# Unit 0 in two halves, and three weights met in plain fp32, in a fused attention and MLP kernel

## The chip, the cores and the metric

The kernel runs on one core of a Trainium2 chip. The metric is the device time of one execution in microseconds (us). The core has five engines that work side by side and meet by semaphores: TensorE (PE, matrix products; PEld is its weight load), VectorE (DVE), ScalarE (ACT), GpSimd (POOL) and SyncE (SP, which here issues the transfers). Each engine takes its instructions strictly in the order in which the program lists them.

## The reference

A linear attention with decay feeds a two-layer MLP.

```python
# r, k, v, w: batch 4, heads 8, steps 768, head size 48; u: heads x 48
for t in range(S):
    cur = einsum('bhd,bhe->bhde', u[None] * kt, vt)
    y[:, :, t] = einsum('bhd,bhde->bhe', rt, state + cur)
    state = wt[:, :, :, None] * state + einsum('bhd,bhe->bhde', kt, vt)
x = y as 3072 tokens x 384
h = x @ w_in                      # 384 x 2048
g = where(h >= 1, h, where(h <= -1, 0, (h + 1)**2 / 4))
out = g @ w_out                   # 2048 x 384
```

The data are fp32; the MLP weights come as 64-bit words and are turned into fp32 on the chip.

## The kernel before

**Units and blocks.** The sequence is cut into 12 units of 64 steps by 4 batches (256 tokens). Two units make a block of 512 tokens; there are six blocks. The eight heads lie as four pairs; a row tile `q` (0 or 1) holds two pairs.

**Attention of a unit** (`attention(u)`). VectorE makes two running products of the decays per row tile with scans (L451 back, L456 forward), and scales `k` (L474, called at L488) and `r` (L474, called at L550) with them. TensorE then makes the scores inside the unit, twice: the diagonal with `u * k` (`among`, tenant `bd`, L508) and the part below it (`among`, tenant `ba`, L508). VectorE copies each set of scores under a mask into `r_` (`picked`, L516). TensorE also transposes `k` (L558), multiplies the scores with `v` (`along`, L618), forms the state update (`umat`, L583), moves the rows of the fourth head pair beside the other three (`spread`, L709, with the permutation `perm` that POOL builds from the constants at L443), and subtracts the rounded part of x (`less`, L699). ScalarE reads x out of PSUM twice, as its high part (L688) and its low part (L684). For units 0 and 1 ScalarE also multiplies `k` with `u` (L479) before the diagonal scores.

**Weights** (`weight(f)`, 16 tiles of 128 hidden columns). A transfer brings the words (L335). ScalarE converts the upper word (L347) into one of three fp32 buffers `fl` and the lower word (L352); VectorE adds signs (L366) and joins both (L369). Then the fp32 tile is split: the high part `w_hi` (L343 on ScalarE, L341 on VectorE for two of them) and the rest `w_lo` (L373, VectorE). A buffer of `fl` is free for the weight three further on when `w_lo` has been made.

**Products** (`products(n)`). Every product of x with a weight is made of three single-pass products of type fp32r: high by high, high by low, low by high. So one weight tile and one block half take nine matmuls into the hidden tile (`product_in`, L1262) and nine out of it (`product_out`, L1282). Between them stand the activation: two ScalarE passes (L1062, L1063), a minimum and maximum on VectorE (L1072), and the split of g into high (L1074, ScalarE) and low (L1075, VectorE). In block 0 the first five weights are done by halves of 256 tokens: for unit 0 the steps (0), (1, 2), (3, 4).

**Order.** The program first lists all operations with their reads and writes. `ORDER` is then a written-out permutation of that list, which fixes the order on every engine; `BANKS` gives each PSUM tenant its bank; `FILLS` names places in TensorE's order where products with a tile of zeros are put in (operation, bank, columns). The first transfers in SP's order are: decays and r, k of row tile 1, decays of row tile 0, decays of unit 1, the mask `below`, r, k of row tile 0, the constants `cst` (seventh), weights 0, 1 and 2, and `v` of unit 0. They are 261.5 KB for the decays of a row tile, 512 KB for its r and k, 32 KB for `below`, 96 KB for `cst`, 768 KB for a weight and 384 KB for `v`. The final three blocks use a scheme with fewer products (L932), which the change leaves as it is.

Of the kernel before, what the change touches and what calls it, by code (L numbers as in the profile page):

```python
# [22 lines left out]
UT = 256  # L23
# [109 lines left out]
)  # L133
FILLS = (
    (42, 0, 256, False), (50, 0, 512, False), (54, 0, 384, False),
)

LOW = 7.499 * 2.0**-32


class Plan:
# [26 lines left out]
    def emits(self, fill):  # L168

        put_in = {n: x for n, *x in FILLS}  # L170
        for n in ORDER:
            if n in put_in:
                fill(*put_in[n])
            self.ops[n]["emit"]()
# [1171 lines left out]
```

## Time and profile before

| | us |
|---|---|
| median of three runs | 486.84 |
| lowest, highest | 486.79, 489.51 |
| profiled execution: span | 489.6 |
| PE busy | 470.8 (96%) |
| PEld busy | 417.4 (85%) |
| DVE busy | 403.1 (82%) |
| ACT busy | 301.8 (62%) |
| POOL busy | 28.1 (6%) |

The page gives the profiled execution's own time only as its span, 489.6 us, near the highest of the three runs. A row of the timeline gives the start, the duration, the engine, the line and the operation; in brackets stands how long the engine had been idle before it and what ended that. Rows of one engine can overlap by a few tenths at their ends, because a matmul or a copy runs out while the next one starts.

### The profile page before, as it was taken

The page shows a single profiled execution, that of the slowest core. Times are in us where ns is not written, and L with a number is a line of the kernel's source. Part 1 is how long each engine was busy: PE and PEld are TensorE (multiplying, and loading weights), DVE is VectorE, ACT ScalarE, POOL GpSimd, SP SyncE. Part 2 cuts the span into 40 slices and gives each one's busy share as a digit, 9 for nine tenths or more (in the row PEclk, how much of TensorE's full clock was granted, in tenths as well). Part 3 has the DMA queues.
Part 4 walks back from the last instruction along what each step waited for, and adds up shares of the span by engine and source line. Part 5 has one row for each costly group of instructions (what it writes and reads, how often), then busy time and mean ns, then how long its engine had stood idle before and what let it go on. Part 6 is the DMA issues. An engine that isn't in the chain of part 4 may idle for free.

```text
span 489.6 us, 13368 instructions
## 1 busy us (share of the span) xinstructions
PE 470.8 (96%) x5709; PEld 417.4 (85%) x5709; DVE 403.1 (82%) x627; ACT 301.8 (62%) x582; POOL 28.1 (6%) x49
## 2 busy tenths in 40 slices
PE   2899999999999999999999999999999999999994
PEld 2689888889999999888888888999889999889984
DVE  6899999999897888798998977889687657585682
ACT  4788988854635276365655567855846656776560
POOL 4000000000000000000000033412300000000000
PEclk9999999999999999999999999999999999999998
DMA  8939646324650435243444201110010111121102
GB/s 317 384 134 325 263 174 205 105 70 147 199 169 3 148 111 170 100 168 105 149 154 138 85 3 50 46 23 15 9 39 28 45 23 21 33 76 44 23 1 72
DMA packets 35205, 53.53 MB, mean 109 GB/s; under 512 B 15744, under 2 KB 22592, under 8 KB 35136
## 3 DMA queue, kind: packets, MB, share of 16 engines
q1 hardware_dynamic: 34992, 52.45, 32.3%
q8 instruction: 47, 0.77, 0.7%
q14 instruction: 22, 0.18, 0.1%
q10 hardware_dynamic: 144, 0.13, 0.1%
HBM read 46.86 MB, written 4.72 MB: 105 GB/s over the span
## 4 chain that ended last, share of the span: by engine, by line
PE 85%; DVE 5%; DMA 5%; issue 2%; SPq 2%; ACT 1%; DVEq 0%
PE ps L1262 37%; PE ps L932 19%; PE ps L1282 18%; PE ps L618 4%; PE ps L508 3%; PE ps L558 2%; DMA rk<-in_rk 2%; DMA wq<-in_w 2%; PE ps L583 2%; DMA nk<-in_nk 1%; DVE y L451 1%; SPq L730 1%; SPq L280 1%; DVE fl L369 1%; DVE rk L474 0%
## 5 line engine op out<-in xcount | busy, mean ns | idle before, releaser
L1262 PE MATMUL ps<-x,wt 128*128 128x512 f32 (+1 forms) x1035 | 214.0, 357 | 0.1
L1262 PEld LDWEIGHTS ps<-x,wt 128*128 128x128 f32 x1035 | 168.1, 188 | 26.8 <-DVE rk L894 0.4
L1282 PE MATMUL ps<-gh,wt 128*128 128x256 f32 (+1 forms) x402 | 79.3, 332 | 0.4 <-DVE g L1072 0.4
L1282 PEld LDWEIGHTS ps<-gh,wt 128*128 128x128 f32 x402 | 61.5, 188 | 7.9 <-DVE g L1072 0.6
L892 ACT ACTIVATE rk<-ps 128x512 f32<-128x512 f32 x48 | 28.4, 597 | 46.3 <-PE ps L1262 27.3
L894 DVE SCALAR_TENSOR_TENSOR rk<-rk,ps 128x512 f32<-128x512 f32 x48 | 32.6, 684 | 24.1 <-ACT rk L893 23.9
L1062 ACT ACTIVATE g<-ps 128x512 f32<-128x512 f32 (+1 forms) x49 | 28.7, 588 | 34.7 <-PE ps L1262 23.1
L1282 PE MATMUL ps<-gl,wt 128*128 128x256 f32 (+1 forms) x201 | 44.1, 328 | 0.0
L1074 ACT CAST gh<-g 128x512 fp32r<-128x512 f32 (+1 forms) x49 | 29.5, 609 | 18.4 <-DVE g L1072 18.4
L1072 DVE SCALAR_TENSOR_TENSOR g<-g,ps 128x512 f32<-128x512 f32 (+1 forms) x49 | 32.2, 665 | 6.3 <-ACT g L1063 6.3
L1075 DVE TENSOR_TENSOR gl<-g,gh 128x512 fp32r<-128x512 f32 (+1 forms) x49 | 32.9, 678 | 4.1 <-ACT gh L1074 3.9
L1282 PEld LDWEIGHTS ps<-gl,wt 128*128 128x128 f32 x201 | 32.3, 188 | 3.6
L451 DVE TENSOR_TENSOR_SCAN y<-wq,ends 128x520 f32<-128x520 f32 x24 | 29.6, 1234 | 5.5 <-POOL r L289 3.8
L900 DVE TENSOR_TENSOR g_again<-rk,nk_again 128x512 fp32r<-128x512 f32 x35 | 24.5, 711 | 11.3 <-ACT nk_again L899 11.2
L900 DVE TENSOR_TENSOR gl<-rk,gh 128x512 fp32r<-128x512 f32 x36 | 25.1, 704 | 9.6 <-ACT gh L899 9.5
L1063 ACT ACTIVATE g<-g 128x512 f32<-128x512 f32 (+1 forms) x49 | 30.0, 622 | 0.4
L893 ACT ACTIVATE rk<-rk 128x512 f32<-128x512 f32 x48 | 29.4, 630 | 0.5
L456 DVE TENSOR_TENSOR_SCAN p<-wq,seeds 128x520 f32<-128x520 f32 x24 | 29.7, 1237 | 0.0
L899 ACT CAST gh<-rk 128x512 fp32r<-128x512 f32 x36 | 22.1, 617 | 7.7 <-DVE rk L918 3.9
L899 ACT CAST nk_again<-rk 128x512 fp32r<-128x512 f32 x35 | 21.5, 617 | 5.7 <-DVE rk L894 3.5
L932 PE MATMUL ps<-nk_again,wt 128*128 128x256 f32 x130 | 24.9, 281 | 0.0
L851 POOL TENSOR_TENSOR p<-wt 128x256 f32<-128x256 f32 x8 | 6.9, 873 | 294.0 <-DVE p L851 294.0
(165 smaller groups left out, 842.5 us busy)
## 6 DMA issues: line engine op xcount, KB each, us to landing
rk<-in_rk SPq DMA_DIRECT2D x18, 512.0 KB, 4.1
wraw<-in_wbits SPq DMA_DIRECT2D x11, 768.0 KB, 6.2
nk<-in_nk SPq DMA_DIRECT2D x9, 768.0 KB, 4.6
wq<-in_w SPq DMA_DIRECT2D x24, 261.5 KB, 3.5
wraw<-in_wbits SPq DMA_DIRECT2D x15, 256.0 KB, 5.9
vn<-in_v SPq DMA_DIRECT2D x9, 384.0 KB, 4.6
rk<-in_rk SPq DMA_DIRECT2D x12, 256.0 KB, 5.8
last<-in_w SPq DMA_DIRECT2D x12, 256.0 KB, 3.0
```

The lines of the kernel that those rows point to most:

```text
L451: V.tensor_tensor_scan(out=y_[:, ::-1], data0=w[:, SEG:0:-1], data1=ends.rearrange("p n c -> p (n c)")[:, ::-1], initial=0.0, op0=ALU.mult ...
L456: V.tensor_tensor_scan(out=pv[:, q].rearrange("p n c -> p (n c)"), data0=w[:, 0:SEG], data1=sv, initial=0.0, op0=ALU.mult, op1=ALU.add)
L894: op("DVE", 0.68, [("b", ht)], [qk], lambda: V.scalar_tensor_tensor(out=gf, in0=gf, scalar=1.0, in1=at(ht), op0=ALU.min, op1=ALU.max))
L899: op("ACT", 0.6, [key], fresh_in(("h", i, k)), lambda: A.copy(spare(k, i), x))
L900: op("DVE", 0.67, [key, ("h", i, k)], fresh_in(("l", i, k)), lambda: V.tensor_tensor(out=spare(k, 3 + i), in0=x, in1=spare(k, i).bitcast(F ...
L932: PE.matmul(at(sums_at[b][i])[:, half * UT : half * UT + UT], lhsT=w[wi], rhs=g[gi], start=(b, i) not in opened, stop=True, skip_group_che ...
L1063: op("ACT", c, (), [("g", gk)], lambda: A.activation(gs, gs, AF.Square))
L1072: op("DVE", 0.15 + 0.53 * k, [("b", ht)], [("g", gk)], lambda: V.scalar_tensor_tensor(out=gs, in0=gs, scalar=1.0, in1=hs(), op0=ALU.min, o ...
L1074: op("ACT", c, [("g", gk)], [("gh", gk)], lambda: A.copy(ghs, gs))
L1075: op("DVE", 0.145 + 0.54 * k, [("g", gk), ("gh", gk)], [("gl", gk)], lambda: V.tensor_tensor(out=gls, in0=gs, in1=ghs.bitcast(F32), op=ALU ...
L1262: nc.tensor.matmul(hp, lhsT=wx[f][:, cs], rhs=xt[:, j, :], start=first and n == 0, stop=n == 8, skip_group_check=not first)
L1282: nc.tensor.matmul(o[j], lhsT=wx[f][:, cs], rhs=gt, start=first and i == 0, stop=stop and i == 2, skip_group_check=True)
```

## The change

It does four things.

- **Unit 0 in halves.** The scores of unit 0, their masked copies and the product with `v` are each made in two halves, first head pairs 2 and 3 (row tile 1), then pairs 0 and 1 (row tile 0). The fourth head pair is then spread before the second half of `along`.
- **Three weights in plain fp32.** For unit 0, weights 0, 1 and 2 are multiplied straight from the fp32 buffers `fl`, with x in fp32 (a new copy `x32`, ScalarE) and g in fp32, three plain fp32 matmuls in and three out in place of nine and nine. The split of g (L1074, L1075) falls away for these two steps. `w_hi` and `w_lo` of these weights are still made, for the other tokens.
- **A new order.** `ORDER` and `BANKS` are new as a whole. Among the first transfers `cst` is now fourth, `v` of unit 0 comes ahead of weight 2, and the decays of unit 1 come tenth. On POOL `seeds` is set second and one half of `r_` only after `perm`.
- **Six fills in place of three**: 1920 columns of zeros in all, where 1152 were. They stand ahead of the transpose of row tile 1 (896 columns), its diagonal scores (128), the first half of `along` (640) and the second half (256), all in unit 0.

```diff
+PARTED = {0}
+PLAIN = {0, 1, 2}
 FILLS = (
-    (42, 0, 256, False), (50, 0, 512, False), (54, 0, 384, False),
+    (46, 3, 512, False), (46, 3, 384, False), (38, 3, 128, False), (54, 0, 512, False), (54, 0, 128, False), (55, 2, 256, False),
 )
...
+        if early and parted:
+            bd = plan.tenant(2)
+            for q in (1, 0):
+                op("PE", 0.48, [("ku", q), "nk", ("r", slot[q])], [("bq", bd, q)], lambda q=q: among(
+                    bd, lambda q: ku[:, q], lambda q: raw(q, 0), mine(q)), code=64, small=True, touch=[bd])
+                op("DVE", 0.7, [("bq", bd, q), "cst"], R_of(q), lambda q=q: picked_of(bd, twice.bitcast(I32), q), touch=[bd])
...
+        if parted and u == 0:
+            op("PE", 0.48, [*R_of(1), vk, ("vpad", 0), rs[1]], [("b", by)], lambda: along((2,)), fresh=False, code=64, small=True)
+            op("PE", 0.48, [*R_of(0), vk, ("vpad", 0), rs[0]], [("bq", by, 0)], lambda: along((0,)), fresh=False, code=64, small=True, touch=[by])
...
+        if u == 0:
+            op("ACT", 0.8, [("b", by), ("bq", by, 0)], ["x32"], lambda: A.copy(
+                x32.rearrange("p a (c g t) -> p a c g t", c=2, g=2), two(by).rearrange("p g (a c t) -> p a c g t", a=4, t=C)[:, 0:3]))
...
+        plain = b == 0 and cs == halves[0] and set(fs) <= PLAIN
+        for i, f in enumerate(fs if plain else ()):
+            op("PE", 1.4, [("fl", f % FULL), "x32", *after], [("b", ht)], lambda i=i, f=f: product_in_f32(
+                nc, at(ht)[:, i * w : i * w + w], fl[f % FULL], x32, not i), fresh=not i, code=12)
...
-            op("ACT", c, [("g", gk)], [("gh", gk)], lambda: A.copy(ghs, gs))
+            if not plain:
+                op("ACT", c, [("g", gk)], [("gh", gk)], lambda: A.copy(ghs, gs))
...
+            if plain:
+                op("PE", 1.4, [("g", gk), ("fl", f % FULL)], [("b", acc[j]) for j in range(3)], fresh=begin, code=12,
+                   emit=lambda f=f, mine=mine, begin=begin: product_out_f32(
+                       nc, [at(t)[:, cs] for t in acc], fl[f % FULL], gs[:, mine], begin))
+                continue
...
+def product_in_f32(nc, hp, s, x, first=True):
+    for n, j in enumerate((2, 0, 1)):
+        nc.tensor.matmul(hp, lhsT=s[:, j * 128 : j * 128 + 128], rhs=x[:, j, :], start=first and n == 0, stop=n == 2, skip_group_check=not first)
```

The numbers in `op(...)` are the planner's own costs; they do not reach the chip.

## Rows read from the trace of the kernel before

**Rows 1.** The page, busy time of each engine (share of the span) and instructions.
```profile
PE 470.8 (96%) x5709; PEld 417.4 (85%) x5709; DVE 403.1 (82%) x627; ACT 301.8 (62%) x582; POOL 28.1 (6%) x49
```

**Rows 2.** Windows: PE, PEld, DVE, ACT, POOL busy (instructions); clock, DMA share, GB/s.
```profile
10.00:20.00 10.00, 9.54 (x219) 6.95 (x218) 8.67 (x12) 7.24 (x13) 1.65 (x2) 1.00 1.02 392
20.00:50.00 30.00, 27.88 (x563) 25.23 (x561) 29.85 (x41) 26.05 (x47) 0.00 (x0) 1.00 0.72 250
50.00:60.00 10.00, 10.00 (x115) 9.13 (x108) 9.47 (x15) 9.05 (x14) 0.00 (x0) 1.00 0.77 309
60.00:100.00 40.00, 40.00 (x426) 33.33 (x425) 39.78 (x57) 31.49 (x52) 0.00 (x0) 1.00 0.46 154
100.00:200.00 100.00, 99.44 (x1643) 93.55 (x1641) 89.48 (x122) 49.92 (x100) 0.00 (x0) 1.00 0.38 124
200.00:480.00 280.00, 279.76 (x2731) 245.59 (x2730) 217.72 (x373) 174.47 (x352) 22.25 (x30) 1.00 0.20 60
```

**Rows 3.** Timeline of PE, 0 to 50 us, lines of the front.
```profile
8.72 1.09 PE L558 MATMUL ps<-cst,xf 128*128 128x128 f32 x4 [8.72 <-DVE xf L474]
...
10.48 1.99 PE L508 MATMUL ps<-rk,nk 64*64 64x64 f32 x64
...
15.23 1.13 PE L298 MATMUL ps<-zero 128*128 128x512 f32 x2
...
18.45 1.58 PE L709 MATMUL ps<-ob,nk 128*128 128x128 f32 x12
...
26.09 0.66 PE L558 MATMUL ps<-cst,rk 128*128 128x128 f32 x4 [0.61 <-DVE rk L474]
...
32.38 0.67 PE L618 MATMUL ps<-rk,st 64*48 64x64 f32 x32
...
38.20 3.39 PE L1262 MATMUL ps<-x,wt 128*128 128x256 f32 x27
41.44 0.87 PE L1282 MATMUL ps<-gh,wt 128*128 128x256 f32 x6
...
49.64 1.33 PE L508 MATMUL ps<-rk,nk 64*64 64x64 f32 x64 [0.63 <-ACT nk L479]
```

**Rows 4.** Timeline of DVE, 12 to 41 us, lines that the change touches or moves.
```profile
12.70 1.31 DVE L516 COPY_PREDICATED r<-cst,ps 128x1024 f32<-128x1024 int32 x1 [0.47 <-ACT wraw L352]
...
15.37 1.30 DVE L516 COPY_PREDICATED r<-below,ps 128x1024 f32<-128x1024 int32 x1 [0.86 <-PE ps L508]
...
22.80 0.56 DVE L341 CAST wt<-fl 128x768 fp32r<-128x768 f32 x1
...
30.35 0.95 DVE L373 TENSOR_TENSOR wt<-fl,wt 128x768 fp32r<-128x768 f32 x1
31.21 1.33 DVE L516 COPY_PREDICATED r<-below,ps 128x1024 f32<-128x1024 int32 x1
...
35.13 0.42 DVE L1072 SCALAR_TENSOR_TENSOR g<-g,ps 128x256 f32<-128x256 f32 x1
...
36.33 0.42 DVE L1075 TENSOR_TENSOR gl<-g,gh 128x256 fp32r<-128x256 f32 x1
...
38.13 0.67 DVE L1072 SCALAR_TENSOR_TENSOR g<-g,ps 128x512 f32<-128x512 f32 x1
...
39.88 0.67 DVE L1075 TENSOR_TENSOR gl<-g,gh 128x512 fp32r<-128x512 f32 x1
```

**Rows 5.** Waits for the constants, POOL's timeline, 8 to 12 us.
```profile
8.72 0.70 POOL L443 COPY nk<-cst 128x32 f32<-128x32 f32 x1 [5.03 <-DMA cst<-in_consts]
```

**Rows 6.** SP's issue of v of unit 0, from the timeline.
```profile
5.93 0.69 SPq L280 DMA_DIRECT2D vn<-in_v  x1
```

**Rows 7.** Transfers issued from 0 to 60 us: count, KB each, us to landing.
```profile
vn<-in_v SPq DMA_DIRECT2D x1, 384.0 KB, 9.4
```

**Rows 8.** Timeline of ACT, 20 to 26 us.
```profile
20.19 0.79 ACT L688 CAST x<-ps 128x768 fp32r<-128x768 f32 x1
...
25.39 0.91 ACT L347 ACTIVATE fl<-wraw 128x768 f32<-128x768 f32 x1 [0.90 <-DVE wt L373]
```

More of the change, by code (lines that the diff above doesn't have):

```diff
@@ L145, in __init__, with add @@
         self.tenants, self.where = [], BANKS
-    def add(self, engine, cost, emit, reads=(), writes=(), port=0, size=0, fresh=True, code=0, small=False):
+    def add(self, engine, cost, emit, reads=(), writes=(), port=0, size=0, fresh=True, code=0, small=False, touch=()):
         n = len(self.ops)
+        for t in touch:
+            self.tenants[t]["users"].append(n)
         deps = {self.writer[x] for x in (*reads, *writes) if x in self.writer}
@@ L168, in emits @@
     def emits(self, fill):
-        put_in = {n: x for n, *x in FILLS}
+        put_in = {}
+        for n, *x in FILLS:
+            put_in.setdefault(n, []).append(x)
         for n in ORDER:
-            if n in put_in:
-                fill(*put_in[n])
+            for x in put_in.get(n, ()):
+                fill(*x)
             self.ops[n]["emit"]()
@@ L288, in attention_moe @@
         for h in range(2):
-            op("POOL", 0.5, (), [("R", h)], lambda h=h: G.memset(r_[:, h], 0.0))
+            op("POOL", 0.5, (), [("R", h, q) for q in range(2)], lambda h=h: G.memset(r_[:, h], 0.0))
     last_f = ob[:, 0:UT]
@@ L394, in bonus @@
             nc.sync.dma_start(out=u_sb[:, cs], in_=a["us"][:, cs])
-    aside_keys = {1: [("aside", 1, 1)], 2: [("aside", 0, 0), ("aside", 0, 1), ("aside", 1, 0)]}
+    x32 = flat(xf[1], 512, 1280).rearrange("p (a t) -> p a t", t=UT)
+    aside_keys = {1: [("aside", 1, 1), "x32"], 2: [("aside", 0, 0), ("aside", 0, 1), ("aside", 1, 0)]}
     def attention(u):
@@ L496, in attention, with among @@
         dv = d_.rearrange("p c (a h) -> p h a c", h=2)
-        def among(to, left, right):
-            for pair in range(4):
+        def among(to, left, right, pairs=range(4)):
+            for pair in pairs:
                 q, pr = divmod(pair, 2)
@@ L511, in among @@
                             )
-        both_R = [("R", 0), ("R", 1)]
+        both_R = [("R", h, q) for q in range(2) for h in range(2)]
         def picked(of, mask):
@@ L518, in picked, with picked_of, R_of, mine @@
                 data=two(of).rearrange("p h (n c) -> p (h n) c", c=C))
-        if early:
+        def picked_of(of, mask, q):
+            V.copy_predicated(
+                out=r_[:, :, 2 * q : 2 * q + 2].rearrange("p h a b c -> p h (a b) c"),
+                mask=mask.unsqueeze(1).unsqueeze(1).broadcast_to([128, 2, 4, C]),
+                data=two(of)[:, :, 256 * q : 256 * q + 256].rearrange("p h (n c) -> p h n c", c=C))
+        def R_of(q):
+            return [("R", h, q) for h in range(2)]
+        def mine(q):
+            return range(2 * q, 2 * q + 2)
+        parted = u in PARTED
+        if early and parted:
[4 more added lines that the diff above has]
+                op("DVE", 0.7, [("bq", bd, q), "cst"], R_of(q), lambda q=q: picked_of(bd, twice.bitcast(I32), q), touch=[bd])
+        elif early:
             bd = plan.tenant(2)
@@ L545, in attention @@
             for h in range(2):
-                op("DVE", 0.68, ["d", "cst"], [("R", h)], lambda h=h: V.tensor_tensor(
+                op("DVE", 0.68, ["d", "cst"], [("R", h, q) for q in range(2)], lambda h=h: V.tensor_tensor(
                     out=r_[:, h], in0=twice.unsqueeze(1).unsqueeze(1).broadcast_to([128, 4, 2, C]),
@@ L558, in ktrans @@
                     PE.transpose(out=at(b)[:, lo : lo + 128], in_=ready(q, 1)[:, tokens(pr, c2)], identity=ident)
-        op("PE", 0.95, [*ks, *rs], [("b", ba)],
-           lambda: among(ba, lambda q: ready(q, 1), lambda q: ready(q, 0)), code=128, small=True)
+        if parted:
+            for q in (1, 0):
+                op("PE", 0.48, [ks[q], rs[q]], [("bq", ba, q)], lambda q=q: among(
+                    ba, lambda q: ready(q, 1), lambda q: ready(q, 0), mine(q)), code=64, small=True, touch=[ba])
+        else:
+            op("PE", 0.95, [*ks, *rs], [("b", ba)],
+               lambda: among(ba, lambda q: ready(q, 1), lambda q: ready(q, 0)), code=128, small=True)
         goes_on = u < NU - 1
@@ L568, in attention @@
                     kt[:, 2 * q : 2 * q + 2].rearrange("p a b c -> p (a b c)"), at(b)))
-        op("DVE", 1.32, [("b", ba), "below"], both_R, lambda: picked(ba, below))
+        if parted:
+            for q in (1, 0):
+                op("DVE", 0.7, [("bq", ba, q), "below"], R_of(q), lambda q=q: picked_of(ba, below, q), touch=[ba])
+        else:
+            op("DVE", 1.32, [("b", ba), "below"], both_R, lambda: picked(ba, below))
         bu = plan.tenant(2) if goes_on else None
@@ L635, in cross, with along @@
             crossed(1)
-        def along():
+        def along(ones=(0, 2)):
             if u:
                 crossed(0)
-            for one_ in (0, 2):
+            for one_ in ones:
                 for c2 in range(2):
@@ L662, in attention @@
                 op("DVE", 0.94, [("b", bu), ("s", now)], [("s", new)], step)
-        op("PE", 1.42 if u else 0.95, [*ss, *both_R, vk, ("vpad", u % 2), *rs], [("b", by)], along, fresh=False, code=192 if u else 128, small=True)
+        if parted and u == 0:
+            op("PE", 0.48, [*R_of(1), vk, ("vpad", 0), rs[1]], [("b", by)], lambda: along((2,)), fresh=False, code=64, small=True)
+            op("PE", 0.48, [*R_of(0), vk, ("vpad", 0), rs[0]], [("bq", by, 0)], lambda: along((0,)), fresh=False, code=64, small=True, touch=[by])
+        else:
+            op("PE", 1.42 if u else 0.95, [*ss, *both_R, vk, ("vpad", u % 2), *rs], [("b", by)], along, fresh=False,
+               code=192 if u else 128, small=True)
         blk, half = divmod(u, 2)
@@ L717, in attention @@
         parts_x = 1 if flat_x else 2
+        if u == 0:
+            op("ACT", 0.8, [("b", by), ("bq", by, 0)], ["x32"], lambda: A.copy(
+                x32.rearrange("p a (c g t) -> p a c g t", c=2, g=2), two(by).rearrange("p g (a c t) -> p a c g t", a=4, t=C)[:, 0:3]))
         for what in (0,) if alone else (1, 0):
-            op("ACT", 0.37 if what else 0.8, [("b", by)], [names(what, 0), *(() if what else aside_keys.get(blk, ()))], lambda w=what: yevac(0, w))
+            op("ACT", 0.37 if what else 0.8, [("b", by), ("bq", by, 0)], [names(what, 0), *(() if what else aside_keys.get(blk, ()))], lambda w=what: yevac(0, w))
             if u not in INPLACE and not flat_x:
@@ L819, in attention_moe @@
     st_keys = [[("spad", i), ("s", i)] for i in range(2)]
-    R_keys = [("R", 0), ("R", 1)]
+    R_keys = [("R", h, q) for q in range(2) for h in range(2)]
     olds = [(("w", 0),), (("w", 1),), (("w", 2),), ("y",), ("seeds",), *[fl_keys] * 4, R_keys, R_keys, *[vn_keys] * 3, *st_keys]
@@ L1057, in products @@
         x = x_[b % 2]
-        for i, f in enumerate(fs):
+        plain = b == 0 and cs == halves[0] and set(fs) <= PLAIN
+        for i, f in enumerate(fs if plain else ()):
+            op("PE", 1.4, [("fl", f % FULL), "x32", *after], [("b", ht)], lambda i=i, f=f: product_in_f32(
+                nc, at(ht)[:, i * w : i * w + w], fl[f % FULL], x32, not i), fresh=not i, code=12)
+        for i, f in enumerate(() if plain else fs):
             op("PE", 2.1 * kw, [("wh", f), ("wl", f), *x_keys(b, cs), *after], [("b", ht)], lambda i=i, f=f: product_in(
@@ L1073, in products @@
                 out=gs, in0=gs, scalar=1.0, in1=hs(), op0=ALU.min, op1=ALU.max))
-            op("ACT", c, [("g", gk)], [("gh", gk)], lambda: A.copy(ghs, gs))
-            op("DVE", 0.145 + 0.54 * k, [("g", gk), ("gh", gk)], [("gl", gk)], lambda: V.tensor_tensor(
-                out=gls, in0=gs, in1=ghs.bitcast(F32), op=ALU.subtract), port=True)
+            if not plain:
+                op("ACT", c, [("g", gk)], [("gh", gk)], lambda: A.copy(ghs, gs))
+                op("DVE", 0.145 + 0.54 * k, [("g", gk), ("gh", gk)], [("gl", gk)], lambda: V.tensor_tensor(
+                    out=gls, in0=gs, in1=ghs.bitcast(F32), op=ALU.subtract), port=True)
         acc = sums_at[b]
@@ L1098, in attention_moe @@
     attention(1)
+    early_steps = [n for n, (b, fs, cs) in enumerate(steps) if b == 0 and cs == halves[0] and set(fs) <= PLAIN]
     for f in range(NF):
         weight(f)
+        for n in early_steps:
+            if steps[n][1][-1] == f:
+                products(n)
     for n, (b, fs, cs) in enumerate(steps):
@@ L1117, in attention_moe @@
                 divided(b + 1)
-        if n < len(steps) - 1:
+        if n < len(steps) - 1 and n not in early_steps:
             products(n)
@@ L1152, in flat, with product_out_f32 @@
     return (t.rearrange(f"p {names} -> p ({names})") if len(t.shape) > 2 else t)[:, lo:hi]
+def product_in_f32(nc, hp, s, x, first=True):
+    for n, j in enumerate((2, 0, 1)):
+        nc.tensor.matmul(hp, lhsT=s[:, j * 128 : j * 128 + 128], rhs=x[:, j, :], start=first and n == 0, stop=n == 2, skip_group_check=not first)
+def product_out_f32(nc, o, s, g, first):
+    for j in range(3):
+        cs = slice(384 + j * 128, 384 + j * 128 + 128)
+        nc.tensor.matmul(o[j], lhsT=s[:, cs], rhs=g, start=first, stop=False, skip_group_check=True)
 def general(tc, a, ident, w_hi, w_lo):
```

161 rows, old and new, of tables (BANKS, ORDER) are left out of this document.

## The prediction, made before the changed kernel was run

> **What bounds the kernel now.** I read the page first: TensorE is busy 96% of the span and VectorE 82% [rows 1]. Such a mean hides stages, so the windows come next. From 100 us on TensorE has no idle time worth speaking of, under 1 us in 380, while VectorE has slack [rows 2]. From 20 to 100 us VectorE is as full as TensorE: 29.85 of 30 us and 39.78 of 40 us [rows 2]. Only the first 20 us have room: VectorE waits 1.33 us between 10 and 20 us [rows 2], and the timeline of TensorE shows an idle head of 8.72 us and short waits up to 26 us [rows 3]. So whatever the change brings must come from the front, and it is kept only as far as VectorE, which feeds TensorE until 100 us, also gets ahead.
>
> The head has a cause that the rows name. TensorE's first product, a transpose, is released together with POOL's first copy from `cst`, and that copy had waited 5.03 us for the transfer of `cst` [rows 3, 5].
>
> **The transfers.** Before `cst` 1841 KB were queued (three tiles of decays, two of r and k, the mask); now it is 1035 KB. The 0.83 MB less, at the 392 GB/s of the window from 10 to 20 us [rows 2], bring `cst` at about 6.6 us, 2.1 us sooner. POOL's three copies from `cst` and the memset of half of `r_` that is moved behind them then end by about 10.4 us at the price of the first copy and some waiting, in time for VectorE's first masked half at 10.5 us. In exchange weight 2 moves back: up to and with it 4625 KB are queued, as many as up to `v` before, which landed 5.93 + 9.4 = 15.3 us [rows 6, 7]. I take 15.3 us for weight 2. Its conversion on ScalarE stands ahead of the reads of x in the new order, so x in fp32 is there at about 18.6 us: 15.3, the conversion 0.9, `u * k` of unit 1 0.9, x high 0.79 and `x32` 0.79 [rows 8].
>
> **VectorE, up to the second masked copy of unit 1.** Before, that copy starts at 31.21 us [rows 4]. In the new order VectorE has the same list ahead of it, apart from these:
> - the waits of 0.47 and 0.86 us ahead of unit 0's masked copies [rows 4]: with halves the scores of row tile 1 are ready while VectorE still works on row tile 0, and weights 0 and 1 are converted before their signs are due. Minus 1.33.
> - the cast and the remainder of weight 2, 0.56 and 0.95 with ends that overlap by 0.09 [rows 4], come later. Minus 1.33.
> - the minimum and maximum of both plain steps come earlier: 0.42 and 0.67, less the overlaps [rows 4]. Plus 0.93.
> - two masked copies of 1.31 become four halves. No row shows a half; at best half the time, at worst the 0.67 of a full-speed row of 512 elements and no overlap [rows 4]. Plus 0.1 (0 to 0.2).
>
> Sum: minus 1.63, the copy starts at 29.6 us. What VectorE no longer does at all are the two remainders of g, 0.42 and 0.67 [rows 4], 0.95 with overlap. Added to the waits and less the 0.1, VectorE can be 2.2 us ahead at 100 us, and 2.9 us if the 0.15 and 0.53 us that it still idles between 20 and 60 us [rows 2] go too.
>
> **TensorE at the same point.** Before, TensorE begins unit 1's product with the scores at 32.38 us [rows 3]; it then has weights 0 to 2 in for unit 0 and nothing out. In the new order two of the three products out stand ahead of this point, worth twice 1.08 us by the 27 matmuls that take 3.24 us from start to start [rows 3]. Not yet done is one transpose (0.66 less the run-out of 0.15, so 0.5) [rows 3].
>
> A plain fp32 product is not in the trace, so it is bounded. Not under the 1.08 us of the nine single passes [rows 3]. One 512-column product with zeros takes 1.13 us [rows 3], so three of 256 columns take at most 1.70. The spread is six plain fp32 matmuls of 128 columns in 1.58 us [rows 3], so three of 256 take 1.58. With the run-out of 0.15 us (3.39 against 3.24) [rows 3] taken off, both give 1.4 to 1.5. I take 1.43, the spread's row being the nearest in kind: 0.35 more for each of the six, 2.1 us in all (0 to 3.7).
>
> Is there room for it? Up to that point TensorE has some 23.5 us of work: unit 0 7.5, unit 1 3.8, five plain products 7.2, 1920 columns of zeros 3.7 at 1.9 ns a column, the first products with zeros 1.3 [rows 3]. It can start at about 2.3 us, when POOL has set the tile of zeros, and has until 30.8. That leaves 5 us for waits (for `cst`, for r scaled, for the min and max). So five of the six dearer products and the 768 more columns of zeros (1.5 us) lie in time that was idle. If that cover were gone they would cost 1.8 and 1.5 us. The sixth product comes later, in full time: plus 0.35.
>
> The sum at this point: the product with the scores starts 1.6 us earlier, 2.16 us of products out lie behind it, one transpose is due (plus 0.5) and one dear product (plus 0.35). TensorE is 2.9 us ahead. The wait of 0.63 us at 49.64 us [rows 3] I leave as it is, since weight 5, which is joined later than before, is the next thing late there. VectorE permits 2.2 to 2.9. **I take 2.6 us.** On ScalarE the casts of g go and one copy of 0.79 us comes [rows 8]; behind that copy stand conversions that VectorE wants only 2 us later. The new order after 100 us is costed at nothing: TensorE's queue is full there [rows 2], so an order can only win the rest of its idle time, 0.8 us, or add waits.
>
> The profiled execution took 489.6 us and would take 487.0; the median of the runs is 2.8 us lower, and the same shift gives 486.84 - 2.6 = **484.2 us**. What this measurement can tell from no change is about 1%, 4.9 us.
>
> **The rivals.**
>
> *Nothing gained.* The change doesn't reach what it is for if x in fp32 comes late. It stands on ScalarE behind a conversion that waits for weight 2, and the transfer engines are full from 10 to 20 us [rows 2], so a transfer that slips by 2 us moves the plain products by 2 us. VectorE's waits return (1.33), the min and max stand in its way, and the shift is about 0.3: 486.5 us. For it speaks the full DMA, against it that TensorE has unit 1's scores to do meanwhile. Chance 0.21.
>
> *Slower: the held buffers.* A plain product out reads `fl`, so weight 3 cannot be converted before it and before the remainder of weight 0. Before, that conversion began at 25.39 us, having waited 0.90 us for the remainder [rows 8]. Now it begins at 28.7 us by VectorE's order, two ScalarE passes follow, and its sign is due on VectorE at 30.8: there is no slack. If each of weights 3, 4 and 5 makes VectorE wait for 1.5 us of its ScalarE pair, 4.5 us are lost where VectorE cannot win them back [rows 2]: 486.84 - 2.6 + 4.5 = 488.7 us. It decides once VectorE idles more than 2.6 us between 28 and 42 us. Against it: in the new order the two engines fit, if only just. Chance 0.14.
>
> *Slower: the clock.* The first group of 64 small products takes 1.99 us where later ones take 1.33 [rows 3], though the row of the window shows a granted clock of 1.00 [rows 2]; the first matmuls are slow. [...] Chance 0.05.
>
> *More gained.* VectorE's limit does not bite, TensorE keeps 2.9, and the waits of 0.63 at 49.64 us [rows 3] and the rest up to 200 us (0.56 us) [rows 2] go: 486.84 - 4.1 = 482.7 us; with plain products at their lower bound up to 0.35 more, since only the sixth lies in full time. Chance 0.12.
>
> **How the numbers follow.** My own case has 0.48. Its range is 483.5 to 485.5 by the bounds of the terms. The range that should hold 8 in 10 reaches over the more-gained case to 481.0 and over the held buffers to 489. Faster by over 1% means under 482.0: a part of the more-gained case and some of my own, 0.11. Slower means over 491.7: the far ends of the two slower cases, 0.06. The rest, 0.83, is within 1%.
>
> **What would show it.** In the new profile: TensorE's first transpose at 6 to 7 us; unit 0's four masked half copies at 0.65 to 0.7 us each; plain products at 0.45 us per matmul of 256 columns; x in fp32 read at about 18 us; the second masked copy of unit 1 near 29.6 us with no VectorE wait over 0.5 us before it; TensorE full from 31 us on. I am wrong if VectorE idles between 28 and 42 us, if the transfer of weight 2 lands after 17 us, or if TensorE shows more than 2 us of idle time after 40 us.

## The result, and the profile after

The change made the kernel slower by about half a per cent. The median is 490.78 us (488.44 to 493.50, 9 runs) against 487.75 us of the kernel before in the same comparison: ratio 1.0059, interval 1.0033 to 1.0085. That is small, but clear of the scatter of the runs. Timed once more it was 490.99 against 488.42 us, ratio 1.0058 (1.0029 to 1.0087). The forecast was 484.2 us, 2.6 us less than before.

The page of the profiled execution after (489.74 us, span 488.2) answers to [rows 1]:

```profile
PE 474.7 (97%) x5697; PEld 418.1 (86%) x5697; DVE 406.6 (83%) x627; ACT 306.3 (63%) x581; POOL 28.1 (6%) x49
```

The windows after, with the columns of [rows 2]:

```profile
10.00:20.00 10.00, 8.52 (x223) 6.43 (x221) 9.47 (x14) 8.01 (x14) 0.00 (x0) 1.00 1.03 391
20.00:50.00 30.00, 28.36 (x522) 24.84 (x522) 29.91 (x41) 26.00 (x45) 0.00 (x0) 1.00 0.90 328
50.00:60.00 10.00, 10.00 (x79) 9.62 (x78) 10.00 (x17) 9.31 (x16) 0.00 (x0) 1.00 0.94 363
60.00:100.00 40.00, 39.29 (x499) 31.78 (x498) 37.93 (x54) 32.23 (x53) 0.00 (x0) 1.00 0.23 74
100.00:200.00 100.00, 99.86 (x1619) 93.96 (x1620) 93.73 (x129) 50.67 (x103) 0.00 (x0) 1.00 0.44 143
200.00:480.00 280.00, 278.41 (x2666) 244.04 (x2659) 216.93 (x365) 175.23 (x346) 22.55 (x30) 1.00 0.18 53
```

TensorE idles 0.71 us between 60 and 100 us, where it was full before, and 1.59 us after 200 us against 0.24 [rows 2]. VectorE idles 2.07 us between 60 and 100 us, against 0.22.

The front of TensorE's timeline after, to be read beside [rows 3]:

```profile
6.29 0.63 PE L588 MATMUL ps<-cst,xf 128*128 128x128 f32 x4 [0.22 <-DMA cst<-in_consts]
...
10.13 0.69 PE L518 MATMUL ps<-rk,nk 64*64 64x64 f32 x32
...
20.22 2.80 PE L1218 MATMUL ps<-xf,fl 128*128 128x256 f32 x12
...
31.79 0.67 PE L657 MATMUL ps<-rk,st 64*48 64x64 f32 x32 [0.93 <-ACT look L697]
```

and of VectorE's, beside [rows 4]; the last row is one of a later stretch:

```profile
10.94 0.73 DVE L531 COPY_PREDICATED r<-cst,ps 128x512 f32<-128x512 int32 x1 [0.36 <-issue]
...
30.39 1.31 DVE L526 COPY_PREDICATED r<-below,ps 128x1024 f32<-128x1024 int32 x1
...
83.55 0.69 DVE L484 TENSOR_TENSOR rk<-rk,y 128x512 f32<-128x512 f32 x1 [2.01 <-DMA rk<-in_rk]
```

The front looks as forecast, only less so: the first transposes 2.4 us earlier than in [rows 3], the second masked copy of unit 1 0.8 us earlier than in [rows 4], where 1.6 was forecast. Unit 1's product with the scores, at which the forecast counted TensorE's lead, starts at 31.79 us against 32.38 in [rows 3]. The loss lies late. Twelve times the kernel loads decays again, 256 KB into one tile named `last`, and ScalarE makes two passes over it that check them (L747 and L748 before, L794 and L795 after). The view of ScalarE's work on that tile gives for each line the count, then the shortest, median and longest duration in ns, then the first and last start. Before:

```profile
L747 ACT ACTIVATE last<-last x12: 617/626/635, 310.9 to 460.8; 128x512 f32<-128x512 f32 x12
```

After:

```profile
L794 ACT ACTIVATE last<-last x12: 626/632/637, 301.4 to 356.9; 128x512 f32<-128x512 f32 x12
```

The new order has them in 56 us instead of 150. The waits after, from 280 to 480 us (who waited for what: sum, times, longest, in us):

```profile
ACT last L794 <- DMA last<-in_w: 8.1, 9, 2.1
PE ps L979 <- DVE g_again L947: 1.3, 1, 1.3
PE ps L1334 <- DVE rk L941: 0.3, 1, 0.3
```

Before, in the same stretch, ScalarE's wait for these transfers and the only wait of TensorE were:

```profile
ACT last L747 <- DMA last<-in_w: 0.2, 1, 0.2
PE ps L932 <- issue: 0.2, 1, 0.2
```

**A measure of progress.** To compare traces whose orders differ, I give each of TensorE's useful matmuls its usual distance from start to start (0.118 us for 256 columns, 0.229 for 512, and so on; zeros count nothing), and look up when a trace has done so much of this work, of 457 us in all. The table is computed from the starts of the matmuls in each trace: the time at which 60 us of work are done, and what the work from 60 to 280, 280 to 360 and 360 to 456.5 us took. To 60 us a plain product counts as 1.07 us, so a few tenths there are the weighting.

| us | 60 done at | 60 to 280 | 280 to 360 | 360 to end | 60 to end |
|---|---|---|---|---|---|
| before, profile shown | 79.9 | 224.3 | 79.9 | 97.8 | 402.0 |
| before, second trace | 78.7 | 225.2 | 79.9 | 97.7 | 402.9 |
| after, first trace | 77.5 | 225.1 | 83.2 | 96.9 | 405.2 |
| after, second | 78.1 | 224.9 | 83.1 | 96.9 | 405.0 |
| after, third | 78.7 | 224.8 | 83.2 | 96.9 | 404.8 |
| after, loads spread (e1) | 78.4 | 223.5 | 80.6 | 98.3 | 402.4 |
| after, no reloads (e6) | 78.4 | 224.7 | 81.6 | 96.9 | 403.2 |
| before with the front of after (h282) | 78.9 | 223.7 | 79.9 | 99.1 | 402.7 |

On the mean of these traces the front gained 1.2 us (79.3 to 78.1) and the rest lost 2.5 us (402.5 to 405.0).

### The profile page after: what moved, and what is told of

Read it like the earlier page. It is cut to its first block, busy times and chain, and to the rows that moved or that the text cites. A ratio compares the mean times of both kernels' runs of the same rounds, so it can differ in the third digit from the quotient of the medians.

```text
span 488.2 us, 13331 instructions
## 1 busy us (share of the span) xinstructions
PE 474.7 (97%) x5697; PEld 418.1 (86%) x5697; DVE 406.6 (83%) x627; ACT 306.3 (63%) x581; POOL 28.1 (6%) x49
## 4 chain that ended last, share of the span: by engine, by line
PE 81%; DMA 7%; ACT 3%; SPq 1%; issue 1%; DVE 1%; ACTq 0%; DVEq 0%
PE ps L1334 35%; PE ps L1354 19%; PE ps L979 16%; PE ps L657 4%; DMA last<-in_w 4%; PE ps L518 2%; PE ps L588 2%; DMA rk<-in_rk 2%; PE ps L622 2%; ACT last L794 1%; ACT last L795 1%; DMA wraw<-in_wbits 1%; SPq L777 1%; DMA xf<-last 0%; SPq L344 0%
## 5 line engine op out<-in xcount | busy, mean ns | idle before, releaser
L1334 PE MATMUL ps<-x,wt 128*128 128x512 f32 (+1 forms) x1008 | 209.4, 359 | 0.3 <-DVE rk L941 0.3
L1334 PEld LDWEIGHTS ps<-x,wt 128*128 128x128 f32 x1008 | 164.9, 188 | 27.3 <-DVE rk L941 1.0
L1354 PE MATMUL ps<-gh,wt 128*128 128x256 f32 (+1 forms) x384 | 76.5, 334 | 0.0
L1354 PEld LDWEIGHTS ps<-gh,wt 128*128 128x128 f32 x384 | 59.1, 188 | 6.9
L1354 PE MATMUL ps<-gl,wt 128*128 128x256 f32 (+1 forms) x192 | 42.7, 330 | 0.0
L1354 PEld LDWEIGHTS ps<-gl,wt 128*128 128x128 f32 x192 | 31.2, 188 | 3.6
L1127 DVE TENSOR_TENSOR gl<-g,gh 128x512 fp32r<-128x512 f32 (+1 forms) x47 | 31.3, 676 | 0.7 <-ACT gh L1126 0.7
```

What stands on the lines that cost most here:

```text
L1127: op("DVE", 0.145 + 0.54 * k, [("g", gk), ("gh", gk)], [("gl", gk)], lambda: V.tensor_tensor(out=gls, in0=gs, in1=ghs.bitcast(F32), op=ALU ...
L1334: nc.tensor.matmul(hp, lhsT=wx[f][:, cs], rhs=xt[:, j, :], start=first and n == 0, stop=n == 8, skip_group_check=not first)
L1354: nc.tensor.matmul(o[j], lhsT=wx[f][:, cs], rhs=gt, start=first and i == 0, stop=stop and i == 2, skip_group_check=True)
```

## The experiments

The expectations call the twelve loads into `last` "reloads of the last weights" in some places; they are reloads of decays. Every ratio is to the kernel before on the same chip.

**The loads crowded and spread.** e1 is the kernel after with the 36 operations of the twelve loads (1138 to 1173) and the four closing ones put back to where the order before has them, counted in TensorE's operations; one PSUM tenant changes its bank.

```diff
-    ... 1206, 1192, 1093, 1220, 1138, 1094, 1225, 1193, 1230, 1210, 1195, 1095, 1194, 1226, 1096, 1214, 1211, 1139, 1247, ...
+    ... 1206, 1192, 1093, 1220, 1094, 1225, 1193, 1230, 1138, 1210, 1195, 1095, 1194, 1226, 1096, 1214, 1211, 1247, ...
```

> The changed kernel, but the twelve reloads of the decays of units 0 to 5 with their two ScalarE passes each (load, absolute value, relu), and the four operations of the final check, stand in the order after as many TensorE operations as they do in the kernel before: spread over 310 to 460 us instead of 301 to 357 us. Theory 'crowded guards': ScalarE stood 8.1 us in front of these reloads in the changed kernel, and the casts of g behind it made VectorE and then TensorE wait; spread out, the waits go and about 3 us come back: 487.5 us, the ratio to the kernel before 0.995 to 1.001, and the times of the runs lie closer together than the 5 us of the changed kernel. Rival 'the front costs more than it gives': the time stays at 490 to 491 us. Rival 'wait for k of unit 3 near 82 us' as the main loss: not touched here, so under 1 us comes back.

Measured: 488.52 us (487.71 to 490.89), ratio 1.0010 (0.9989 to 1.0031). ScalarE waits once, 0.2 us, for these transfers. By the ratios (1.0059 to 1.0010, with intervals that do not meet) 2.4 us of the loss went with the crowding, where 3 were expected. Two pairs, each timed together on one chip, agree: 490.99 us (after) and 488.67 us (f5), 491.35 us (g1) and 488.24 us (g2). The first of each pair has the loads crowded; the second has them spread, with the further small changes described below.

e3 does the reverse to the kernel before: its loads stand as close as the new order has them.

> The kernel before, with nothing changed but the place of the same twelve reloads and their ScalarE passes: after as many TensorE operations as in the changed kernel, so crowded into some 55 us. Theory 'crowded guards': 2 to 4 us slower than the kernel before, about 490.5 us, with ScalarE waiting 5 us or more for the transfers into the tile last. Rival 'the front': no difference, within 0.5 us of the kernel before.

Measured: 500.84 us, ratio 1.0252 (1.0214 to 1.0289), so 12.8 us where 2 to 4 were expected. Its waits from 280 to 480 us:

```profile
ACT last L747 <- DMA last<-in_w: 8.5, 5, 3.4
ACT last L747 <- DMA out_y<-ob: 4.3, 1, 4.3
...
PE ps L1262 <- DVE rk L894: 5.1, 2, 4.9
PE ps L932 <- DVE kt_again L910: 2.1, 1, 2.1
PE ps L1262 <- DVE xf L1007: 1.0, 1, 1.0
```

The same wait for the tile is there, but the loss is far larger. TensorE's waits in this stretch come to 8.8 us, and the clock adds to them: the mean granted clock is 0.990 to 0.993 in its six runs, and 0.997 to 1.000 in the nine of after. In its trace TensorE stood still for 4.89 us, up to 324.13 us, and the granted clock was 0.50 from 322.4 to 329.2 us and 1.00 on both sides of that. The same nine matmuls at 0.50 and at 1.00:

```profile
324.13 4.21 PE L1262 MATMUL ps<-x,wt 128*128 128x512 f32 x9 [4.89 <-DVE rk L894]
...
330.04 2.23 PE L1262 MATMUL ps<-x,wt 128*128 128x512 f32 x9
```

That is some 2.5 us more (an estimate: half of the 5.1 us that TensorE worked at 0.50). The trace of after shows no fall before 486.4 us, when its products are done. So e3 shows that the crowding costs time, and not how much it costs in the kernel after. That the other passes of this order were not fitted to it may be why the waits are longer; no run shows it. e6 asks whether it is the transfer or ScalarE's work that is too much. It is the kernel after without eleven of the transfers; the other operations keep their order:

```diff
-                    load(w.rearrange("p (n c) -> p n c", c=C), a["w"][u, q][:, 0:SEG]...
+                    if i == 0:
+                        load(w.rearrange("p (n c) -> p n c", c=C), a["w"][u, q][:, 0:SEG]...
```

> The changed kernel without eleven of the twelve transfers of decays into the tile `last`; the two ScalarE passes over that tile stay where the new order has them, so from the second on they work on what the tile holds. Theory (the loss between 300 and 360 us is the wait for a transfer into the only tile): ScalarE's 8 us of standing there are gone, TensorE's waits of 1.3 us at 323 us too, and the time is 488.5, as with the passes spread out. Rival (twelve times 1.5 us of ScalarE's own passes crowded into 56 us are too much): ScalarE is late all the same and the time stays at 490 or more.

Measured: 488.58 us (486.95 to 490.33), ratio 1.0017 (0.9994 to 1.0040). The two passes still stand between 301.9 and 362.1 us, and from 280 to 480 us there is left:

```profile
ACT last L791 <- DMA last<-in_w: 0.4, 1, 0.4
PE ps L976 <- DVE g_again L944: 0.4, 1, 0.4
```

So most of it is the wait for a transfer into the only tile: the next load may be issued once ScalarE's second pass has read the tile, then takes 2.9 us (the median of eleven in the trace of after), and ScalarE stands in front of it, with the conversions that TensorE needs behind it in its order. How much it costs is less sure than that it does. The interval of e6 still meets that of after. By the table the work from 280 us on takes 177.7 us before and 180.1 after on the mean, 178.9 in e1 and 178.5 in e6. So in their single traces e1 and e6 win back 1.2 and 1.6 us of the 2.4 lost there, and the rest stays with other parts of the new order; the ratios put the gain at 2.4 and 2.0 us.

**The same kernels once more.** The profiled execution on which the forecast rests has a span of 489.6 us. The later medians of the same kernel are 487.35 to 488.73 us, and in the other profiled executions the time is 1.5 to 1.6 us over the span. Was that execution a fair one to forecast from?

> The kernel before, unchanged, for a second trace. The theory (the profiled execution of before that the forecast rests on was an odd one, 1.5 us above the median of its kind): this trace shows a span of about 486.5 us, and the 2.4 us that the changed kernel led by at 57 us is about 1 us against this one, the difference lying in the first 20 us or after the last product. The rival (that execution is typical, and the lead is lost later, in the order): this trace stands within 0.5 us of the first one at 57 us and at the last matrix product.

> The changed kernel, unchanged, for a second trace. Both theories: ScalarE again stands 6 to 10 us on the transfers of the last weights between 300 and 360 us, and TensorE waits 1 to 3 us there. If the front is not what varies, the second block product of unit 0 ends within 0.5 us of the first trace's; if the front varies by over 1 us from run to run, it shows here.

> The changed kernel, unchanged, timed beside the repaired one. Theory: ratio 1.005 to 1.006 to the kernel before, 490.5 where that takes 488; in the trace ScalarE stands about 8 us on the transfers into `last`, TensorE 1.2 us at 323 us, and the last product ends at 482.7 to 483.1. Rival (the 0.6% was a matter of that one set of runs): ratio 1.003 or less.

The second trace of before has a span of 486.8 us and took 488.35; its runs took 488.38 in the median. TensorE's first waits in it:

```profile
PE ps L558 <- DMA cst<-in_consts: 8.6, 1, 8.6
PE ps L508 <- DVE g L1072: 1.5, 1, 1.5
PE ps L558 <- DVE rk L474: 0.5, 1, 0.5
```

The wait of 0.63 us at 49.64 us of [rows 3] is not there, and another of 1.5 us stands at 178 us, which the first trace does not have. At 60 us of work the second trace is 1.2 us ahead of the first. The theory and the rival were each half right: the lead against a second trace is 0.0 to 1.2 us instead of 1.2 to 2.4, but the last products end within 0.3 us of each other. The two further traces of after show the same wait for `last` (8.5 us in the third) and TensorE waiting 1.2 and 1.5 us, so the loss is no accident of one execution. The ratio of the third, 1.0058, is as expected; its last product, at 483.5 us by the table, comes 0.4 us later than expected.

**The front alone.** h282 takes the operations and the order of after up to place 282 of the order, and goes on in the order of before.

> The changed kernel's operations (halves, plain fp32, six fills) in its own order for the first 282 operations, to about 60 us; everything after that in the order and the banks of the kernel before. Theory 'the front gives what was forecast': TensorE is 2 to 2.5 us ahead at 60 us and keeps it: 2.4 us faster than the kernel before, about 485.3 us, ratio 0.995. Rival 'the front costs more than it gives': equal to or slower than the kernel before, ratio 1.000 to 1.006.

Measured: 488.51 us (487.26 to 489.56), ratio 1.0003 (0.9983 to 1.0024): the front earns nothing that this can tell. The trace shows one wait that comes from the seam:

```profile
71.39 1.15 PE L619 MATMUL ps<-vn,kt 64*64 64x48 f32 x64 [1.03 <-DVE r L523]
```

so the test is not a clean one, and e1 is the better witness: there the front is whole, and its ratio is 1.0010.

f1 is the kernel before with the constants loaded fourth instead of seventh, and nothing else:

```diff
-    1, 0, 14, 6, 9, 5, 7, 15, 3, 16, 2, 56, 19, 4, 22, 17, 8, 18, 27, ...
+    1, 0, 14, 6, 9, 5, 7, 15, 3, 16, 18, 2, 56, 19, 4, 22, 17, 8, 27, ...
```

> The kernel before with one load moved: the constants go right after the third tile of decays, ahead of unit 1's decays, the mask and the second tile of r and k. Theory (VectorE is what the front is worth, and it can win only its own waits ahead of unit 0's masked copies): the first transposes start 2.1 us earlier, at about 6.5 us; VectorE's two waits of 0.24 and 0.62 us (0.47 and 0.86 in the first trace) shrink to under 0.3 together; the second masked copy of unit 1 starts 0.6 to 0.9 us earlier, at 30.1, and the time falls by as much, to about 487.5 against 488.2. Rival (what TensorE gains counts in full): 2 us less, 486.2.

Measured: 487.34 us against 487.35, ratio 0.9995 (0.9972 to 1.0018). The interval holds the theory's 0.7 us as well as no gain at all, but not the rival's 2 us. The transposes start at 6.25 us, 2.3 us earlier than in the second trace of before; VectorE still waits 0.69 us ahead of its second masked copy, and that of unit 1 starts at 30.55 us. TensorE's early start counts only as far as VectorE follows: 60 us of work are done at 78.6 us.

e5 leaves all the products with zeros out (`FILLS = ()`).

> The changed kernel without its six fills of zeros (1920 columns of products with zeros left out; nothing else differs). [...] Rival 'the zeros cost': up to 1.5 us faster than the changed kernel.

Measured: 491.35 us, ratio 1.0058 (1.0029 to 1.0087), as the kernel after. The transposes take 1.09 us and the first scores 1.13, where the rows after have 0.63 and 0.69:

```profile
6.51 1.09 PE L586 MATMUL ps<-cst,xf 128*128 128x128 f32 x4 [2.64 <-DMA cst<-in_consts]
7.53 1.13 PE L516 MATMUL ps<-rk,nk 64*64 64x64 f32 x32
```

and 60 us of work are done at 79.6 us, 1.5 later than the mean of after, but the time is not measurably longer than that of after nor, as the rival had it, shorter. f4 takes e1 and lets POOL set the tile of zeros first, so that the zeros start at 1.24 us and not at 2.21.

```diff
-    1, 14, 15, 2, 16, 4, 0, 18, 22, 11, ...
+    0, 1, 14, 15, 2, 16, 4, 18, 22, 11, ...
```

> The changed kernel with its reloads spread out, and POOL sets the tile of zeros first instead of third after the marks and seeds, so TensorE's products with zeros begin about 1 us earlier. Theory (in most runs TensorE is still slow when the constants land, since the zeros start late and run into the transposes): the zeros start at 1.3 us, the four first transposes take 0.63 us in place of 1.06 and start at 6.3, the first masked half starts 0.6 us earlier than the 11.55 us of the run with the reloads spread, and the time is 488.0 against 488.5. Rival (VectorE finds its next wait): the time is the same within 0.2.

Measured: 489.31 us (487.44 to 490.12), ratio 1.0033 (1.0012 to 1.0053), no better than e1 and slower than the kernel before. The transposes take 0.63 us, as expected, but the first half copy starts at 11.23 us, 0.3 us earlier than in e1, where 0.6 was expected; 60 us of work are done at 77.7 us, 0.7 earlier than in e1. That is lost by 100 us of work, to a wait of VectorE:

```profile
DVE rk L481 <- DMA rk<-in_rk: 1.8, 1, 1.8
```

**A load in the wrong place on SP's queue.** The wait is for k of row tile 0 of unit 3. In the new order its load stands behind one of r that waits for TensorE. e4 is e1 with these two exchanged; f5 is e4 with the tile of zeros first.

```diff
-    ... 203, 259, 276, 262, ... 265, 205, 275, 386, ...
+    ... 203, 259, 275, 276, 262, ... 265, 205, 386, ...
```

> The changed kernel with its twelve reloads of the last weights spread out, and with the load of the first row tile of k of unit 3 issued before the load of r on SP's queue. Theory (VectorE's stand of 2.0 us at 82 us costs TensorE 0.7 us for good): that stand is under 0.5 us, the lead at 100 us is 0.7 us more than with the reloads spread alone, and the time is 487.8, against 488.5. Rival (the stand is hidden, since VectorE has 20% idle after it): the time stays within 0.3 us of 488.5.

> The changed kernel with three repairs together: the reloads into `last` spread out, the load of k of unit 3 ahead of the load of r, and the tile of zeros set first. Theory (the lead of the front, where the constants land early, was lost at 82 us to VectorE's stand for k of unit 3): VectorE does not stand there, the 40 us of TensorE's work from 78 to 119 us take 40.5 us and not 41.5 as with the zero tile alone, the last product ends at 480.2, and the time is 1.0 us under the kernel before, ratio 0.998. Rival (such a lead is lost to the next wait): the last product ends at 481 or later and the ratio is 1.001 to 1.003.

Measured: e4 488.65 us, ratio 0.9997 (0.9977 to 1.0017); f5 488.67 us, ratio 1.0008 (0.9984 to 1.0032). VectorE does not stand there any more. The row of f5 that answers to the one at 83.55 us after:

```profile
81.65 0.68 DVE L481 TENSOR_TENSOR rk<-rk,y 128x512 f32<-128x512 f32 x1
```

The work from 60 to 100 us takes 40.5 us (41.5 in f4, 41.8 in the first trace of after), as the theory had it. But the next wait took the gain, 0.7 us of TensorE for `rk` at 166 us, and by the same measure the last product was done at 481.1 us, where 480.2 was expected: the rival was right on the time. The ratios of e1, e4 and f5 are too close for their intervals to tell apart.

**Two halves that wait for each other.** In the traces of the new front the first masked half copy starts 0.12 to 0.13 us after the *other* half's scores end. In the second trace of after, TensorE:

```profile
6.65 1.06 PE L588 MATMUL ps<-cst,xf 128*128 128x128 f32 x4
...
10.89 0.69 PE L518 MATMUL ps<-rk,nk 64*64 64x64 f32 x32
```

and VectorE:

```profile
11.71 0.74 DVE L531 COPY_PREDICATED r<-cst,ps 128x512 f32<-128x512 int32 x1 [1.16 <-issue]
```

g1 exchanges the two in the list, which leaves each engine's own order as it is:

```diff
-    ... 66, 48, 64, 40, 105, 39, 43, ...
+    ... 66, 48, 64, 39, 40, 105, 43, ...
```

> The changed kernel with one pair exchanged in `ORDER`: the masked copy of the diagonal scores of row tile 1 (operation 39, VectorE) is listed ahead of the diagonal scores of row tile 0 (operation 40, TensorE). The order on each engine stays as it is. Theory (the copy of the first half waits for the scores of the second half, since it is listed behind them and both lie in one PSUM tenant): the copy starts right after VectorE's scan, at 10.6 us, with no idle time ahead of it, where it started 0.12 us after the second scores in the traces so far, at 10.9 to 11.9; the second masked copy of unit 1 starts 0.4 to 1.1 us earlier, near 30.0; the time is 490.2. Rival (the copy waits for something else that ends then, POOL's memset or a pass of ScalarE): it still starts at 10.9 or later.

> The same exchange in the kernel with three repairs. Theory: the first masked half starts at 10.6 us, the second masked copy of unit 1 at 30.1 (30.64 without the exchange), TensorE has done its first 60 us of work at 77.3 (77.8 without), and the time is 0.5 us less, 488.1 against 488.7; ratio 0.998 to 1.000. Rival (what VectorE wins goes into its next wait): the second copy at 30.6, the same time.

g1: 491.35 us, ratio 1.0054 (1.0029 to 1.0078); g2, which has the exchange on top of f5: 488.24 us, ratio 0.9994 (0.9973 to 1.0016). VectorE in g1, with its first half copy, a later wait, and the second masked copy of unit 1:

```profile
10.42 0.70 DVE L528 COPY_PREDICATED r<-cst,ps 128x512 f32<-128x512 int32 x1
...
17.97 0.69 DVE L481 TENSOR_TENSOR rk<-rk,y 128x512 f32<-128x512 f32 x1 [0.52 <-ACT nk L486]
...
30.36 1.30 DVE L523 COPY_PREDICATED r<-below,ps 128x1024 f32<-128x1024 int32 x1
```

and TensorE's scores of the other half in it:

```profile
11.18 0.69 PE L515 MATMUL ps<-rk,nk 64*64 64x64 f32 x32 [0.50 <-DVE r L528]
```

The copy starts without idle time, so it had waited for the scores because they were listed ahead of it. Now the scores wait for the copy: in one PSUM tenant the two halves exclude each other, whichever comes first. Only the list was changed, and no engine's order, so the wait is one that the program sets. What VectorE wins at 10 us it loses by 18 us to ScalarE's `u * k` (0.52 us; 0.64 us for another ScalarE pass at 21.64 in g2), and the copy of unit 1 starts where it did. Theory right on the cause, rival right on the time. No version ran measurably faster than the kernel before.

## Why the prediction was wrong

**The step that failed most** is the sentence "the new order after 100 us is costed at nothing ... an order can only win the rest of its idle time, 0.8 us, or add waits". It saw that an order can add waits and put a zero on it, from a full queue on TensorE [rows 2]. That says how little there is to win, nothing of what may be lost. The order put twelve loads through one tile into a third of the time they had. By the ratios of e1 and e6 this costs 2.0 to 2.4 us; by the table it is 3.3 us between 280 and 360 us, of which 0.9 come back where before has these loads, and e1 and e6 win back 1.2 and 1.6 of the 2.4 that are left. The change as shown did not tell it, since the order is a list of numbers; the places of the load, the passes and their tile in it could have been looked up.

**VectorE's sum of minus 1.63 us** was the second. Its list of work was right: the cast and remainder of weight 2 fell behind the copy, both plain minimum and maximum came ahead of it, and a half copy takes 0.73 us (0.65 to 0.7 forecast). The term that failed is the 1.33 us of waits that were to go. "The scores of row tile 1 are ready while VectorE still works on row tile 0" holds for the work and not for the PSUM tenant, so a wait of 0.36, 1.16 and 0.78 us stands ahead of the first half copy in the three traces of after. The second masked copy of unit 1 came at 30.39, 30.99 and 30.81 us; before it came at 31.21 and 30.84. That is 0.3 us on the mean, not 1.63. The 1.33 us were also those of one trace: in the second trace of before these waits are 0.86 us. TensorE's sum took its 1.6 us from here. Unit 1's product with the scores begins at 31.79, 32.37 and 32.21 us after, and began at 32.38 and 32.00 us before, so 0.1 us earlier on the mean. The other terms of that sum leave 2.16 - 0.5 - 0.35 = 1.3 us.

**TensorE 2.6 us ahead** became 1.2 by the table's means, near that 1.3. Against the trace shown it would have been nearly right for the first trace of after (79.9 to 77.5). But 1.2 us of that was the trace of before: the wait that the forecast left as it is [rows 3] was an accident of that execution, with some tenths of the first transfers. Then 0.9 to 1.6 us by the same measure went between 60 and 100 us of work, where VectorE stood for a load behind a waiting one on SP's queue. This is the prediction's own condition, that a gain is kept only as far as VectorE also gets ahead. Of the 6.6 us between forecast and result, 0.9 us is the base: the forecast set out from a median of 486.84 us of three runs, and nine runs give 487.75.

**What held.** The constants: TensorE's first transpose at 6.29 us (6 to 7 forecast). x in fp32: read from 18.64 us (18.6). Weight 2 was converted from 16.23 us, having waited 1.66 us for its transfer, 0.9 later than the 15.3 forecast and under the bound of 17. The plain product: the twelve instructions of two products in, two to a matmul, took 2.80 us, so 1.3 to 1.4 us per product (1.43 taken). The held buffers did not bite: VectorE is busy 29.91 of the 30 us from 20 to 50 us. Of the forecast's signs of being wrong one came, by a little: TensorE idles 2.1 to 2.4 us between 40 and 480 us in the three traces of after (1.4 and 1.9 in the two of before). Nor is it full from 31 us on, as forecast: it idles 0.8 to 1.7 us up to 60 us.

**The rivals.** "Nothing gained" (0.21) is nearest for the front, though by another way than a late x. "The clock" (0.05) may have a small part: in the second trace of after the four transposes took 1.06 us, in the first 0.63, and in e5, without zeros, each half of the scores takes 1.1 us up to 16 us, where it takes 0.69 after. The windows give a granted clock of 1.00 there, as [rows 2] does from 10 us on, but that is no reading. The trace's record of the clock begins only at 14.0 us in the first trace of before, at 5.1 and 8.0 us in the first two of after and at 18.7 us in e5, each time at 1.00, and the windows count what lies ahead of it as 1.00. Ahead of it the same work takes 1.5 to 1.7 times as long as later: 1.99 against 1.33 us for 64 scores and 1.09 against 0.66 for four transposes in [rows 3], 1.06 against 0.66 for these in the second trace of after. In e3 nine matmuls took 1.9 times as long at 0.50 as at 1.00. So no run shows what the clock was in the first microseconds, on which the forecast's 0.06 for slower drew in part; the runs show the longer times, and e5 shows that they decide nothing measurable here. The forecast's own case had 0.48, the slower cases 0.19 together, and neither of these had the mechanism that decided.

**What stays open.** By the table after is 1.4 us behind before at its last product, while the medians differ by 2.6 to 3.0 us (interval of the ratio: 1.6 to 4.1 us). The span goes on for 5.0 to 5.5 us after the last mark in most traces and for 6.8 to 7.7 us in some of either kernel, while the last stores land, so single traces scatter by about that. And e1's last product comes 0.8 us before that of the second trace of before, without a shorter median.

## What to carry to other kernels

Before a new order is costed at nothing, look up each buffer that is filled over and over, and see how close its turns now stand: one tile, a transfer of 3 us and two passes need a turn of 5 us (after, the transfer took 2.9 us and the passes 1.5, and the twelve loads were issued 4.8 us apart on the mean), however idle the engines look. When a step is halved, look whether the waits can tell the halves' buffers apart: here they could not, and halves in tenants of their own were not tried. And a gain of 2 us in a kernel full of close deadlines has to be measured against two or three traces of before, since one trace has its own accidental waits of that size.

## What the runs showed of the hardware that was not expected

The same transfer of 96 KB of constants, fourth in the queue, landed 3.7 to 5.6 us after its issue, so TensorE's first transpose moved between 6.2 and 8.1 us from trace to trace of the kernels that have it there. A load of 256 KB into `last` near 453 us took 2.9 to 3.0 us in three traces; near 443 us it took 3.0 us in the second trace of before, 4.0 in e4, 4.2 in e1 and 5.2 in h282 (issued at 442.76 us), where ScalarE stood 0.9 us for it. A plain fp32 matmul of 256 columns shows as two instructions of 0.22 us from start to start, 1.8 times as long as one single-pass matmul of that width per instruction and 3.7 times per matmul (0.118 us).
